# Two MLP groups of two batches recast as 2x2 blocks with Strassen's seven products, and the last expert products of batch 2 at the lowest priority

## The chip, the cores and the metric

The kernel runs on one core of one Trainium2 chip. The metric is the device time of one execution in microseconds (us). TensorE (PE) multiplies matrices into the eight banks of its accumulator memory (PSUM, the tile `bank`); VectorE (DVE), ScalarE (ACT) and GpSimd (POOL) do the elementwise work, and SyncE (SP) issues the transfers. All on-chip data lie in one tile, `arena`.

## The reference, cut to what matters

Three stages follow one another for 4 batches of 448 positions and 768 features: causal attention with 12 heads, an MLP with a low-rank mix over positions, and a top-2 mixture of 4 small attention experts. The change is in the two MLP products.

```python
u  = x + (x^T @ U @ V)^T                       # low-rank mix over the 448 positions
ch = np.maximum(u @ w_ch1, 0.0) @ w_ch2        # 768 -> 3072 -> 768
x  = u + ch
...
out += mask[..., None] * w[:, :, kk:kk + 1] * (a @ v @ wo[e])   # experts
```

## The kernel before, in words

**Numbers.** A float32 value is split into two float16 halves, high and low, and a product of two values is three float16 products (`PASS`: high by high, high by low, low by high). A product of a 768-long contraction is thus 6 blocks of 128 by 3 passes, 18 matmuls of 128x128 by 448 columns into one bank.

**The MLP.** The 3072 hidden features are cut into 4 groups (`NG`) of 6 blocks (`GF`). `mlp(g, bs)` makes the 6 hidden blocks of group g for the batches bs: 18 matmuls each, then ACT applies relu in the bank, ACT casts the high half, DVE subtracts for the low half (`HID`). Then come the 6 output blocks, 18 matmuls each, which DVE adds to the running sum `X3[b]`. Group 2 of batches 2 and 3 is the step `m223`, group 3 the step `m323`: each 24 products of 18 matmuls.

**The weights** come as raw 8-byte words from `in_w1`/`in_w2` (both shown as `in_w_dram`). `weight_tile` decodes each of 48 tiles on DVE, scales it on ACT (high half into a slot of `ring`, full precision in `DEC`), lets POOL make the low half and writes both halves to a scratch tensor in HBM, `W16` (shown as `w`). Later uses reload the tile from there, 384 KB each.

**The steps** stand in the string `ORDER`: `a2` is attention of batch 2, `m02` MLP group 0 of batch 2, `e2` the experts of batch 2. Before, the end of it is `... a3 m02 m12 m223 m323 e2 m03 m13 e3`.

**The order on the engines** is not the order of the code. `Program` records every instruction with a key (`prog.key`); `issue` then runs a list schedule with costs of its own and, on each engine, takes the ready instruction with the lowest key. Attention has low keys; MLP products have `FILL`, the highest, and so fill PE between the attention's products; evacuations have `URGENT`. The experts' products have 0.6e6. The result is one fixed row of instructions on each engine: on the chip each engine waits in that row.

**Scales.** Casts need a power-of-two scale from the largest value. `lowrank` writes a row maximum of each feature block; `split_u` reduces them over the partitions with two small PE products and DVE steps (`reduce_all`) and then casts. Batch 0 uses a bound known beforehand (`CAP`). In `mlp`, the last of group 3 (`g == NG - 1`) takes the maxima anew, which `experts` uses.

Of the kernel before, what the change touches and what calls it, by code (L numbers as in the profile page):

```python
# [23 lines left out]
KD = D // 128  # L24
# [21 lines left out]
SM = 400  # L46
NE = 6
ORDER = "a0 a1 m00 m01 m101 m20 m30 e0 a2 m21 m31 e1 a3 m02 m12 m223 m323 e2 m03 m13 e3"
# [233 lines left out]
def kernel(  # L282
# [40 lines left out]
    bank = banks.tile([128, 8, 512], F32, name="bank")  # L323
    prog.pitch = {bass.MemoryType.SB: total // 4 * 4, bass.MemoryType.PSUM: 8 * 2048}
    W16 = nc.dram_tensor("w16", (NT, 128, 1536), F16, kind="Internal").ap()
    prog.scratch = [W16.tensor]
    BANKS = {"s": (0, 1), "o": (2,), "l": (3, 4), "m": (5, 6, 7), "f": (5, 6), "g": (5, 6, 0, 1), "r": (7,), "x": (5, 6), "y": (2, 7), "b": (3, 4)}
# [7 lines left out]
    def mm(o, lhsT, rhs, start, stop):  # L335
        pe.matmul(o, lhsT, rhs, start=start, stop=stop)
# [21 lines left out]
    def tslot(r, o):  # L358
# [8 lines left out]
        (P32[0:3], PHL[0:2], PT[0:3]), (P32[0:3], PHL[0:2], PT[0:3]),  # L367
# [29 lines left out]
    SCAP = small(1)  # L397
    RF0 = small(NG * GF)
# [193 lines left out]
    def lowrank(n):  # L592
# [19 lines left out]
        if not b:  # L612
            split(UH[0][:, p], UL[0][:, p], X3[0][:, p], SCAP)

    def split_u(b, cast=True):
        t = TMP[:, 7:8]
        dve.tensor_reduce(out=t, in_=AMX[:, b * KD:(b + 1) * KD], axis=AX.X, op=ALU.max)
        reduce_all(t, PU[:, b:b + 1], SU[:, b:b + 1])
# [3 lines left out]
    HT = 4500.0  # L622

    def attention(b):
        if not b:
            prog.key = 0.0
            v_scale(b)
            dve.tensor_tensor(out=CAP, in0=PV[:, 0:1], in1=GAIN, op=ALU.mult)
            dve.tensor_scalar(bits(SCAP), bits(CAP), EXPM, None, op0=ALU.bitwise_xor)
            dve.tensor_scalar(SCAP, SCAP, 2.0 ** 12, None, op0=ALU.mult)  # L630
        for p in range(NP):
# [20 lines left out]
        split_u(b, b > 0)  # L652
# [15 lines left out]
    def weight_tile(i, first):  # L668
# [23 lines left out]
        dve.tensor_scalar(s, s, 2.0 ** 58, None, op0=ALU.mult)  # L692
# [5 lines left out]
        sp.dma_start(out=W16[i], in_=both)  # L698

# [34 lines left out]

    def factors(g):
# [6 lines left out]
        dve.tensor_scalar(TS[:, 7:8], CAP, SU[:, 0:1], 2.0 ** -13, op0=ALU.mult, op1=ALU.mult)  # L742
        dve.tensor_scalar(RF0[:, g * GF:(g + 1) * GF], rf, TS[:, 7:8], None, op0=ALU.mult)

    def mlp(g, bs):

        if 0 in bs:
            factors(g)
# [289 lines left out]
```

## Time and profile before

| What | Value |
|---|---|
| Time, median of 3 runs | 1097.61 us (1097.33 to 1097.76) |
| Span of the profiled execution, first to last instruction | 1094.4 us |
| PE busy | 1064.8 us, 97% of the span |
| DVE, ACT, POOL busy | 607.4, 596.5, 350.4 us |

The profiled execution's own time is known as its span alone; the median stands 3.2 us above it. An engine's busy time is the union of its instructions; matmuls overlap in the pipeline, so the count of matmuls in a stretch tells more than their mean duration. "Idle before" is the engine's idle time just ahead of an instruction, and the name behind it is what ended that time. All instructions of the scheduler bear the line L252, so groups are told apart by shape.

### The profile page before, as it was taken

To read this page: it belongs to the slowest core of one execution; us is meant where nothing else is said; L and a number is where in the kernel's file an instruction comes from. 1 tells how busy PE (TensorE), PEld (TensorE's weight loads), DVE (VectorE), ACT (ScalarE), POOL (GpSimd) and SP (SyncE) were. 2 spreads that over 40 slices of the span, in tenths; PEclk is the share of its full clock that TensorE was granted. 3 is DMA by queue.
4 is the path that set the end of the run, shared out by engine and by line. 5 is a ranking of instruction groups with operands and counts; after the bars stand their busy time and mean duration, and the time that the engine had idled before them with its cause. 6 is when DMAs were issued, how large, how long until landed. Compare 5 with 4: busy or idle time off the path is not lost.

```text
span 1094.4 us, 18802 instructions
## 1 busy us (share of the span) xinstructions
PE 1064.8 (97%) x6932; PEld 568.5 (52%) x6932; DVE 607.4 (56%) x1711; ACT 596.5 (55%) x1445; POOL 350.4 (32%) x411
## 2 busy tenths in 40 slices
PE   8999999999999999999999999999999999999996
PEld 3555554555555555644455644455555555655554
DVE  6788798868786875454546454444112135422253
ACT  3998998666755662567772566762310311731253
POOL 2786767334453420235540225540000000310011
PEclk9999999999999999999999999999999999999998
DMA  5999899647676664449993538984111111555023
GB/s 175 240 242 230 220 208 241 211 164 228 227 234 229 218 242 163 115 120 233 235 202 104 121 112 187 232 170 120 58 58 58 58 58 58 130 134 162 15 41 95
DMA packets 213228, 173.68 MB, mean 159 GB/s; under 512 B 175536, under 2 KB 178736, under 8 KB 213136
## 3 DMA queue, kind: packets, MB, share of 16 engines
q1 hardware_dynamic: 213136, 172.48, 59.2%
q8 instruction: 54, 0.88, 0.3%
q14 instruction: 38, 0.31, 0.1%
HBM read 102.72 MB, written 26.74 MB: 118 GB/s over the span
## 4 chain that ended last, share of the span: by engine, by line
PE 45%; DMA 7%; ACT 3%; DVE 1%; issue 1%; POOL 0%; SPq 0%; POOLq 0%; ACTq 0%
PE bank L252 45%; DMA arena<-arena 7%; ACT arena L252 3%; DVE arena L252 1%; DMA out_dram<-arena 0%; POOL arena L252 0%; ACT bank L252 0%; SPq L252 0%; POOLq L252 0%; ACTq L252 0%
## 5 line engine op out<-in xcount | busy, mean ns | idle before, releaser
L252 PE MATMUL bank<-arena 128*128 128x448 f16 (+10 forms) x6496 | 979.4, 327 | 23.8 <-DMA arena<-arena 11.5
L252 PEld LDWEIGHTS <-arena 128*128 128x128 f16 (+4 forms) x5960 | 486.9, 105 | 433.6 <-issue 81.2
L252 POOL TENSOR_TENSOR arena<-arena 128x384 f16<-128x384 f32 (+6 forms) x400 | 348.2, 891 | 733.5 <-ACT arena L252 708.7
L252 ACT ACTIVATE arena<-arena 112x112 f32<-112x112 f32 (+12 forms) x799 | 433.7, 579 | 228.2 <-DVE arena L252 192.7
L252 DVE TENSOR_TENSOR arena<-bank,arena 128x448 f16<-128x448 f32 (+2 forms) x160 | 95.4, 602 | 190.7 <-ACT arena L252 167.5
L252 DVE CUSTOM_DVE_ANT_0 arena<-bank,arena 112x112 f32<-112x112 f32 (+4 forms) x280 | 125.2, 476 | 71.5 <-PE bank L252 58.1
L252 ACT ACTIVATE bank<-bank,arena 128x448 f32<-128x448 f32 x96 | 57.6, 603 | 178.7 <-PE bank L252 177.6
L252 DVE SCALAR_TENSOR_TENSOR arena<-arena 128x768 int32<-128x768 int32 (+6 forms) x159 | 150.8, 965 | 6.4 <-ACT arena L252 5.7
L252 DVE SCALAR_TENSOR_TENSOR arena<-bank,arena 128x448 f32<-128x448 f32 (+1 forms) x120 | 73.6, 615 | 134.2 <-PE bank L252 113.9
L252 ACT ACTIVATE arena<-bank 128x448 f16<-128x448 f32 (+2 forms) x160 | 82.6, 523 | 45.6 <-PE bank L252 43.5
L252 DVE TENSOR_SCALAR arena<-arena 128x1 int32<-128x1 int32 (+10 forms) x367 | 85.4, 255 | 35.1 <-ACT arena L252 19.5
L991 PE MATMUL bank<-arena 128*128 128x448 f16 x436 | 95.7, 361 | 2.0 <-DVE arena L922 1.0
L252 PEld LDWEIGHTS bank<-arena 64*112 64x112 f32 (+5 forms) x536 | 48.6, 174 | 41.2 <-issue 15.6
L991 PEld LDWEIGHTS <-arena 128*128 128x128 f16 x436 | 40.8, 102 | 46.8 <-issue 14.2
L252 DVE TENSOR_REDUCE arena<-arena 128x1 f32<-128x448 f32 (+6 forms) x107 | 57.8, 545 | 3.8 <-DMA arena<-in_we_dram 2.5
L252 ACT ACTIVATION_READ_ACCUMULATOR arena<-arena 112x1 f32 (+1 forms) x304 | 57.4, 189 | 0.0
L252 ACT ACTIVATE arena<-bank,arena 64x128 f16<-64x128 f32 (+2 forms) x85 | 34.1, 406 | 40.3 <-PE bank L252 37.4
L252 DVE DVE_READ_ACCUMULATOR2_ANT arena<- 112x1 f32 (+1 forms) x280 | 23.0, 82 | 0.1
L252 DVE TENSOR_TENSOR arena<-arena 112x8 f16<-112x8 f32 (+6 forms) x77 | 22.2, 304 | 1.0
L252 DVE CAST arena<-arena 112x8 f16<-112x8 f32 x32 | 14.6, 462 | 2.7 <-PE bank L252 2.5
L252 DVE TENSOR_SCALAR arena<-bank 128x1 f32<-128x1 f32 x48 | 7.3, 152 | 13.5 <-PE bank L252 11.5
L252 DVE COPY arena<-bank 128x1 f32<-128x1 f32 (+2 forms) x14 | 2.2, 158 | 10.0 <-PE bank L252 10.0
(12 smaller groups left out, 18.6 us busy)
## 6 DMA issues: line engine op xcount, KB each, us to landing
arena<-w SPq DMA_DIRECT2D x114, 384.0 KB, 3.2
arena<-in_w_dram SPq DMA_DIRECT2D x48, 768.0 KB, 5.0
w<-arena SPq DMA_DIRECT2D x54, 384.0 KB, 3.6
arena<-in_qk_dram SPq DMA_DIRECT2D x24, 448.0 KB, 4.2
arena<-in_v_dram SPq DMA_DIRECT2D x24, 224.0 KB, 4.5
out_dram<-arena SPq DMA_DIRECT2D x24, 224.0 KB, 2.1
arena<-in_we_dram SPq DMA_DIRECT2D x6, 384.0 KB, 5.8
arena<-arena SPq DMA_TRANSPOSE x88, 4.7
```

Source lines behind the costliest of these rows:

```text
L252: fn(*a, **k)
L991: prog.idle = lambda: nc.tensor.matmul(bank[:, 7, 64:512], ZERO.to_broadcast([128, 128]), ZERO.to_broadcast([128, S]), start=True, stop=True)
```

## The change

**The blocks.** Groups 2 and 3 are done by `strassen(g)` for batches 2 and 3 together. A unit takes two blocks of features by the two batches: the weights are a 2x2 matrix of blocks (even and odd contraction blocks by two output blocks), the activations another (even and odd contraction blocks by batch 2 and batch 3). `seven` makes the four result blocks from seven products of 9 matmuls each (3 contraction pairs by 3 passes) in place of eight. A group has three hidden units and three output units, 63 matmuls each.

**The sums.** Four of the seven need sums of weight blocks (`stationary`: four POOL operations on 128x3x128 elements and two casts a unit, from a full-precision copy `W32` in HBM that `weight_tile` now writes too, for the 24 tiles of these groups) and sums of activations (`operands` for the input, made once; `hidden_unit` for the hidden blocks). `stationary` holds two units' blocks in `ring`.

**The results** are put together on DVE, ACT and POOL: in `hidden_unit` from the banks through `HB` to `BH`, in `output_unit` straight into `X3` and two accumulators.

**Around it.** Batches 2 and 3 share one scale known beforehand (`CAP2`, `SCAP2`), so batch 3 is cast block by block in `lowrank`. Attention of batch 3 gets four buffers in place of two for the transposed weights (`PHL` and two in `hid`). The maxima for the experts are taken by the last group in `ORDER` that adds to a batch (`LAST`): group 3 for batch 2, group 1 for batch 3. The six output products of the experts of batch 2 get the key `2 * FILL`. `ORDER` ends in `... a3 m02 m12 s2 s3 e2 m03 m13 e3`.

```diff
-ORDER = "a0 a1 m00 m01 m101 m20 m30 e0 a2 m21 m31 e1 a3 m02 m12 m223 m323 e2 m03 m13 e3"
+ORDER = "a0 a1 m00 m01 m101 m20 m30 e0 a2 m21 m31 e1 a3 m02 m12 s2 s3 e2 m03 m13 e3"
...
+             "w": (5, 6, 7, 0, 1, 3, 4, 2)}
...
-        (P32[0:3], PHL[0:2], PT[0:3]), (P32[0:3], PHL[0:2], PT[0:3]),
+        (P32[0:3], PHL[0:2], PT[0:3]),
+        (P32[0:3], PHL[0:2] + [hslot("hid", 10752 + 5120 * i) for i in range(2)], PT[0:3]),
...
+        if b == B - 1:
+            split(UH[b][:, p], UL[b][:, p], X3[b][:, p], SCAP2)
...
         sp.dma_start(out=W16[i], in_=both)
+        if g in JOINT:
+            sp.dma_start(out=W32[i], in_=t)
...
-                if g == NG - 1:
+                if (g, b) in LAST:
                     absmax(AMX[:, b * KD + d:b * KD + d + 1], X3[b][:, d])
...
+    def stationary(n):
...
+        for j in range(2):
+            sp.dma_start(out=f[j], in_=W32[i + j])
+        for j in range(2):
+            sp.dma_start(out=a[j].rearrange("p l k m -> p (l k m)"), in_=W16[i + j])
...
+        pool.tensor_tensor(out=o1, in0=e1, in1=o1, op=ALU.add)
+        pool.tensor_tensor(out=e1, in0=e0, in1=e1, op=ALU.subtract)
+        pool.tensor_tensor(out=e0, in0=o1, in1=e0, op=ALU.subtract)
+        pool.tensor_tensor(out=o0, in0=o0, in1=e0, op=ALU.subtract)
+        for j in (1, 0):
...
+            act.activation(hi, f[j], AF.Copy)
+            low(dve, lo, f[j], hi)
...
+        for x, y, out, first in (
+            ("a11", "11", "1", True), ("s1", "t1", "x", True), ("s2", "t2", "y", True),
+            ("a12", "21", "1", False), ("s4", "22", "x", False), ("s3", "t3", "y", False),
+            ("a22", "t4", "z", True),
+        ):
...
+    def hidden_unit(g, u):
...
+            if x == "a11":
+                act.activation(e1, t, AF.Copy)
+            elif x == "s1":
+                act.activation(e5, t, AF.Copy)
+            elif x == "s2":
+                dve.tensor_tensor(out=h12, in0=t, in1=e1, op=ALU.add)
+            elif x == "a12":
+                act.activation(h11, t, AF.Relu, scale=rf[0])
+            elif x == "s4":
+                dve.tensor_tensor(out=h12, in0=t, in1=h12, op=ALU.add)
+                act.activation(h12, h12, AF.Relu, scale=rf[0])
+            elif x == "s3":
+                dve.tensor_tensor(out=e1, in0=t, in1=e1, op=ALU.add)
+                pool.tensor_tensor(out=e5, in0=e5, in1=e1, op=ALU.add)
+                act.activation(e5, e5, AF.Relu, scale=rf[1])
+            else:
+                dve.tensor_tensor(out=h21, in0=t, in1=e1, op=ALU.add)
+                act.activation(h21, h21, AF.Relu, scale=rf[1])
...
+        cut(dve, "11", h11)
+        pool.tensor_tensor(out=t1, in0=h12, in1=h11, op=ALU.subtract)
+        cut(pool, "t1", t1)
+        cut(dve, "22", h22)
+        pool.tensor_tensor(out=t2, in0=h22, in1=t1, op=ALU.subtract)
+        cut(pool, "t2", t2)
+        cut(dve, "21", h21)
+        pool.tensor_tensor(out=t3, in0=h22, in1=h12, op=ALU.subtract)
+        cut(pool, "t3", t3)
+        pool.tensor_tensor(out=t4, in0=h21, in1=t2, op=ALU.subtract)
+        cut(pool, "t4", t4)
...
-        prog.key = base
+        prog.key = 2 * FILL if b == B - 2 else base
         for d in range(KD):
```

The row of POOL, from the end of attention of batch 3 (`128x448` there: low halves of its results) to the first softmax of the experts of batch 2 (`112x112`). Before:

```order
L252 TENSOR_TENSOR arena<-arena 128x448
L252 TENSOR_TENSOR arena<-arena 112x4x112
L252 TENSOR_TENSOR arena<-arena 128x448
L252 TENSOR_TENSOR arena<-arena 112x112 x2
L252 TENSOR_TENSOR arena<-arena 112x2x112 x2
```

The same place after the change, its second group alone: `128x3x128` are the weight sums of `stationary`, `128x448` the sums and low halves of `hidden_unit`, and the last `128x448` the last sums of `output_unit`.

```order
L252 TENSOR_TENSOR arena<-arena 128x448 x7
L252 TENSOR_TENSOR arena<-arena 128x3x128
L252 TENSOR_TENSOR arena<-arena 128x448 x2
L252 TENSOR_TENSOR arena<-arena 128x3x128
L252 TENSOR_TENSOR arena<-arena 128x448 x9
L252 TENSOR_TENSOR arena<-arena 128x3x128
L252 TENSOR_TENSOR arena<-arena 128x448 x6
L252 TENSOR_TENSOR arena<-arena 128x3x128
L252 TENSOR_TENSOR arena<-arena 128x448
L252 TENSOR_TENSOR arena<-arena 128x3x128 x2
L252 TENSOR_TENSOR arena<-arena 128x448
L252 TENSOR_TENSOR arena<-arena 128x3x128 x3
```

Where POOL had nothing between the two steps, the change puts 69 operations of 128x448 and 48 of 128x3x128 in all (of the latter, four already among attention of batch 3); the weight sums of the output units stand among and behind the hidden units' sums.

The row of DVE around the last MLP products of batch 3 (`SCALAR_TENSOR_TENSOR arena<-bank,arena 128x448` adds one to `X3`) and the start of its experts (`SCALAR_TENSOR_TENSOR arena<-arena 128x448` is the low half of a cast, `TENSOR_TENSOR arena<-bank,arena` the first projection's). Before, each sum is followed by its cast:

```order
L252 SCALAR_TENSOR_TENSOR arena<-bank,arena 128x448
L252 SCALAR_TENSOR_TENSOR arena<-arena 128x448
L252 SCALAR_TENSOR_TENSOR arena<-bank,arena 128x448
L252 SCALAR_TENSOR_TENSOR arena<-arena 128x448
L252 TENSOR_TENSOR arena<-bank,arena 128x448 x2
```

After it, the maximum is taken behind each sum, and the reduction over the partitions stands between the last sum and the first cast:

```order
L252 SCALAR_TENSOR_TENSOR arena<-bank,arena 128x448
L252 TENSOR_REDUCE arena<-arena 128x1 x2
L252 TENSOR_REDUCE arena<-bank 1x1
L252 TENSOR_SCALAR arena<-arena 1x1 x2
L252 COPY arena<-bank 128x1
L252 TENSOR_SCALAR arena<-arena 128x1 x6
L252 SCALAR_TENSOR_TENSOR arena<-arena 128x448 x6
L252 TENSOR_TENSOR arena<-bank,arena 128x448 x2
```

The reduction stood far ahead of this place before; now all six casts wait for it. On PE, 30 of the 36 matmuls of the experts' output products of batch 2 stand in this place after the change, around the reduction's two small products, and the other 6 between the first projections of batch 3; before, all 36 stood among the products of group 0 of batch 3.

The row of SP at the same place: `out_dram<-arena` stores the expert results, six for each batch. Before, those of batch 2 stand ahead of the last weight loads:

```order
L252 DMA arena<-w 128x1536 x2
L252 DMA out_dram<-arena 128x448 x4
L252 DMA arena<-w 128x1536 x3
L252 DMA out_dram<-arena 128x448 x2
L252 DMA arena<-w 128x1536 x7
L252 DMA_TRANSPOSE arena<-arena 128x20x112 x4
```

After it they stand behind them, ahead of the last four transposes:

```order
L252 DMA arena<-w 128x1536 x9
L252 DMA out_dram<-arena 128x448 x6
L252 DMA_TRANSPOSE arena<-arena 128x20x112 x4
L252 DMA out_dram<-arena 128x448 x6
```

The stores of batch 2 are the last thing in SP's row before the softmax transposes of the experts of batch 3.

## Rows read from the trace of the kernel before

**Rows 1.** The page: span, busy time of PE, its granted clock in 40 slices.

```profile
span 1094.4 us, 18802 instructions
...
PE 1064.8 (97%) x6932; PEld 568.5 (52%) x6932; DVE 607.4 (56%) x1711; ACT 596.5 (55%) x1445; POOL 350.4 (32%) x411
...
PEclk9999999999999999999999999999999999999998
```

**Rows 2.** Busy time by stretch: length, busy us of each engine (instructions), clock, DMA share, GB/s.

```profile
250.00:400.00 150.00, 149.44 (x825) 80.83 (x823) 118.89 (x261) 96.41 (x154) 66.08 (x57) 1.00 0.70 234
500.00:760.00 260.00, 251.07 (x1849) 132.77 (x1848) 128.04 (x428) 156.02 (x438) 98.09 (x128) 0.99 0.75 174
760.00:1048.00 288.00, 288.00 (x1635) 152.41 (x1633) 86.56 (x200) 75.19 (x161) 13.30 (x18) 1.00 0.27 76
1048.00:1095.00 47.00, 35.95 (x276) 22.12 (x274) 21.43 (x76) 22.36 (x68) 7.79 (x10) 0.89 0.36 79
```

**Rows 3.** Groups of PE by shape between 780 and 880 us.

```profile
L252 PE MATMUL bank<-arena 128*128 128x448 f16 x531 | 100.6, 352 | 0.0
```

**Rows 4.** Timeline of POOL from 700 us: start, duration, idle before.

```profile
747.42 1.03 POOL L252 TENSOR_TENSOR arena<-arena 128x448 f16<-128x448 f32 x1 [9.21 <-ACT arena L252]
937.25 0.40 POOL L252 TENSOR_TENSOR arena<-arena 112x112 f16<-112x112 f32 x1 [188.80 <-ACT arena L252]
```

**Rows 5.** Groups of POOL by shape, 930 to 1094 us: busy, mean ns, idle.

```profile
L252 POOL TENSOR_TENSOR arena<-arena 128x448 f16<-128x448 f32 x4 | 4.1, 1031 | 28.3 <-ACT arena L252 28.3
```

**Rows 6.** Groups of POOL by shape, 210 to 400 us.

```profile
L252 POOL TENSOR_TENSOR arena<-arena 128x384 f16<-128x384 f32 x70 | 80.0, 1163 | 111.1 <-ACT arena L252 109.6 <-PE bank L252 1.4
```

**Rows 7.** Groups by shape over the whole span: DVE and ACT.

```profile
L252 DVE TENSOR_TENSOR arena<-bank,arena 128x448 f16<-128x448 f32 x112 | 68.9, 623 | 145.2 <-ACT arena L252 144.7
L252 DVE SCALAR_TENSOR_TENSOR arena<-bank,arena 128x448 f32<-128x448 f32 x96 | 65.3, 682 | 114.5 <-PE bank L252 113.9
...
L252 DVE TENSOR_TENSOR arena<-arena 112x448 f16<-112x448 f32 x2 | 1.3, 644 | 0.0
L252 DVE SCALAR_TENSOR_TENSOR arena<-arena 128x768 f16<-128x768 f32 x6 | 5.8, 1014 | 0.2 <-ACT arena L252 0.2
...
L252 ACT ACTIVATE arena<-arena 128x768 f16<-128x768 f32 x102 | 89.6, 886 | 53.3 <-DVE arena L252 47.6 <-PE bank L252 5.3
L252 ACT ACTIVATE arena<-arena 128x448 f16<-128x448 f32 x80 | 46.9, 623 | 95.7 <-DVE arena L252 95.4
```

**Rows 8.** The page's DMA issues: engine, count, KB each, median us to landing.

```profile
arena<-w SPq DMA_DIRECT2D x114, 384.0 KB, 3.2
```

**Rows 9.** PE by stretch of 4 us: length, busy (instructions), clock, DMA share, GB/s.

```profile
688.00:692.00 4.00, 1.99 (x26) 1.00 1.20 316
692.00:696.00 4.00, 4.00 (x14) 0.57 0.88 296
```

**Rows 10.** Timeline at the end of group 3, the reduction for the experts of batch 2.

```profile
919.16 0.68 DVE L252 SCALAR_TENSOR_TENSOR arena<-bank,arena 128x448 f32<-128x448 f32 x1 [1.50 <-PE bank L252]
...
923.67 3.46 ACT L252 ACTIVATE arena<-arena 128x448 f16<-128x448 f32 x6 [40.21 <-DVE arena L252]
...
924.74 0.68 DVE L252 SCALAR_TENSOR_TENSOR arena<-arena 128x448 f16<-128x448 f32 x1
```

**Rows 11.** Timeline at the start of the experts of batch 3.

```profile
1046.23 0.68 DVE L252 SCALAR_TENSOR_TENSOR arena<-arena 128x448 f16<-128x448 f32 x1 [0.74 <-ACT arena L252]
...
1049.47 9.14 PE L252 MATMUL bank<-arena 128*128 128x448 f16 x60 [0.72 <-DVE arena L252]
```

**Rows 12.** Timeline of POOL, the low half of the last weight tile.

```profile
394.75 1.79 POOL L252 TENSOR_TENSOR arena<-arena 128x384 f16<-128x384 f32 x2 [2.77 <-ACT arena L252]
```

**Rows 13.** Timeline of DVE, the last sum of group 3 for batch 0.

```profile
429.95 0.68 DVE L252 SCALAR_TENSOR_TENSOR arena<-bank,arena 128x448 f32<-128x448 f32 x1 [2.63 <-PE bank L252]
```

More of the change, by code (lines that the diff above doesn't have):

```diff
@@ L333, in psum, with mm @@
         return bank[:, b[used[kind] % len(b)], :]
[L335 to L336 removed]
+    def mm(o, lhsT, rhs, start, stop, **more):
+        pe.matmul(o, lhsT, rhs, start=start, stop=stop, **more)
     UH = [view("uh", b % 2 * 5376, 128, F16, KD * S).rearrange("p (k s) -> p k s", k=KD) for b in range(B)]
@@ L397 @@
     SCAP = small(1)
+    CAP2 = small(1)
+    SCAP2 = small(1)
+    RF1, RF2 = [small(NG * GF) for _ in range(2)]
+    CF2 = [small(KD) for _ in range(2)]
     RF0 = small(NG * GF)
@@ L651, in attention @@
         lowrank(n)
-        split_u(b, b > 0)
+        split_u(b, b == 1, b < B - 1)
+        if b == B - 2:
+            bound(CAP2, SCAP2, PV[:, 2:3], PV[:, 3:4])
+            for k in range(KD):
+                split(UH[b][:, k], UL[b][:, k], X3[b][:, k], SCAP2)
     ring_n = [0]
@@ new lines, in chain, with cut @@
+    def chain(t, terms, first):
+        more = {} if first else {"skip_group_check": True}
+        prog.key = FILL
+        for i in range(0, len(terms), 3):
+            with prog.group():
+                for j, (l, r) in enumerate(terms[i:i + 3]):
+                    mm(t, l, r, first and i + j == 0, i + j == len(terms) - 1, **more)
+        prog.key = URGENT
+    def hidden_unit(g, u):
+        n = 6 * g + u
+        fs = [g * GF + 2 * u + j for j in range(2)]
+        rf = [RF2[:, f:f + 1] for f in fs]
+        e1, e5, h11, h12, h21 = HB[n % 2]
+        banks_ = {}
+        for x, out, first, terms in seven(n, BU):
+            if first:
+                banks_[out] = psum("w")[:, 0:S]
+            t = banks_[out]
+            chain(t, terms, first)
+            if x == "a11":
[16 more added lines that the diff above has]
+                act.activation(h21, h21, AF.Relu, scale=rf[1])
+        h22, t1, t2, t3, t4 = e5, e1, h11, h12, h21
+        def cut(eng, name, x):
+            hi, lo = BH[name][u]
+            act.activation(hi, x, AF.Copy)
+            low(eng, lo, x, hi)
+        cut(dve, "11", h11)
[9 more added lines that the diff above has]
+        cut(pool, "t4", t4)
@@ L972, in moe @@
             for i in range(NE):
-                k = slot()
-                tiles[48 + i] = halves(k)
-                sp.dma_start(out=view("ring", k * 3072, 128, F16, 1536), in_=W16[48 + i])
+                if b == B - 2 and i > 3:
+                    a = view("stage", (i - 4) * 3072, 128, F16, 1536)
+                    tiles[48 + i] = a[:, 0:768], a[:, 768:1536]
+                else:
+                    k = slot()
+                    a = view("ring", k * 3072, 128, F16, 1536)
+                    tiles[48 + i] = halves(k)
+                sp.dma_start(out=a, in_=W16[48 + i])
         else:
```

172 lines of the change are left out of this document (156 added, 16 removed).

## The prediction

> **What bounds the kernel now.** I read the page first: PE is busy for 1064.8 of 1094.4 us [rows 1], but matmuls overlap in the pipeline, so I asked stretch by stretch whether PE runs at its own pace. The stretches show three kinds of time [rows 2]. From 250 to 400 us PE is full while DVE is at 79% (weights are decoded). From 500 to 760 us, attention of batches 2 and 3, PE idles 260 - 251.07 = 8.9 us. From 760 to 1048 us PE is busy for all 288 us; POOL works 13.3 us of it and the DMA share is 0.27. From 1048 us on, the experts of batch 3, everything waits in turn (PE 35.95 of 47 us).
>
> The change falls into the third stretch: `m223` and `m323` fill most of its first half. The groups of PE from 780 to 880 us show 531 matmuls of 448 columns [rows 3], one per 100 / 531 = 188.3 ns with no idle time before any. A matmul removed there is worth 188.3 ns, as long as what replaces it keeps PE fed. POOL's timeline shows how empty the other side is: between 748.5 and 937.25 us it does nothing for 188.8 us [rows 4].
>
> **The change, part by part.**
>
> *Products.* Before: 2 groups x 24 products x 18 = 864 matmuls. After: 12 units x 7 x 9 = 756. The 108 fewer, at 188.3 ns, are **-20.3 us**. A unit is 63 x 0.1883 = 11.86 us of PE; this is the clock against which the other engines must work.
>
> *DVE and ACT.* A hidden unit gives DVE four sums out of the banks (0.623), three low halves (nearest row 112x448 from arena, 0.644) and two weight low halves (0.644 x 768/448 = 1.10 by elements; a 128x768 cast's low half took 1.01): 6.6 us. An output unit gives it eight sums at 0.682 and two low halves, 7.7 us. ACT has 13 operations near 0.623 and two at 0.886 in a hidden unit, 9.9 us [rows 7]. All lie under 11.86 us, so beside PE: 0 by throughput.
>
> *POOL.* A hidden unit needs nine operations of 448 elements and four of 384: 5568 elements a partition. In the quiet end of the program 448 elements took 1.031 us, 2.30 ns each [rows 5]; in the decode stretch 384 took 1.163, 3.03 ns each [rows 6]. A unit thus costs 12.8 to 16.9 us, against PE's 11.86: POOL is behind by 0.9 to 5.0 us for each hidden unit. An output unit needs the four weight sums alone (four of 384, 3.5 to 4.7 us) and lets POOL catch up. Which rate? DVE was busy 21.43 of 47 us (46%) at the quiet end and 79% in the decode stretch [rows 2]; here 6.6 of 11.86 is 55%, about a quarter of the way: 2.49 ns, 13.9 us a unit, 2.0 us behind. Three units are 6 us late, and two groups 12 us. Much of that is covered: in the order on PE, output products that need only plain casts stand forward among the last hidden ones, and the output units of the first group mix with the hidden units of the second. The second group's output products have nothing behind them but `m03`. I take **+5.0 us**, most of it there; bounds 0 and 6 units x 5.0 = 30.
>
> *Transfers.* A unit loads four tiles of 384 KB; before, one such tile served 36 matmuls, 6.8 us of PE. 1.57 MB in 11.86 us is 133 GB/s, while the decode stretch moved 234 GB/s [rows 2]: no bound by rate. But `ring` holds two units, and a load may start only when the unit before last is done; it lands 3.2 us later [rows 8]. PE's order pulls first products of a unit forward, so I expect two such waits of about 1 us, at the starts of a group and of the output units: **+2.0 us**, bounds 0 and 4 x 3.2 = 12.8 if each switch between hidden and output units shows a whole landing.
>
> *Clock.* Where PE idled for half of 4 us (busy 1.99), the next 4 us were granted 0.57 of full speed, a mix of 1.2 and 2.4 GHz [rows 9]: 4 x 0.43 = 1.7 us lost. The waits above make one such fall likely: **+1.7 us**, bounds 0 and three falls, 5.1.
>
> *Full-precision copies.* 24 writes of 384 KB join the weight stage. DMA there is at a share of 0.70 for 234 GB/s [rows 2]; 9.4 MB at the implied full rate of 334 GB/s is 28 us of the 16 engines, in some 120 us of slack 0.30, so it fits but makes loads later. What hides it is the lead of the weights: the last tile was ready at 396.5 us [rows 12], and its product's sum came at 429.95 [rows 13], 3.4 us of products after its start, a lead of 30 us, or 1.2 us for each of the 24 tiles. **0**; if the cover went, each tile's 1.2 us beyond that would be paid by PE, so I keep 5 as the upper end.
>
> *Attention of batch 3.* Two more buffers, casts that no longer wait for a reduction, and some of POOL's new work standing among its softmax. PE's idle time in the whole stretch is 8.9 us [rows 2]; I take **0**, between -3 and +3.
>
> *The end.* The experts of batch 2 lose 36 matmuls (6.8 us) from the full stretch, and the same 36 stand where batch 3 now waits for its maximum. That wait is priced by the same chain for batch 2: last sum at 919.16, first cast 923.67, its low half done at 924.74 + 0.68 = 925.42, so 6.3 us from the end of the last product [rows 10]. The order puts 30 matmuls there, 5.65 us: about 0.6 us of PE idle is new. Before, that chain ran far ahead, and PE then stood 0.72 us at 1049.47, right after the last low halves [rows 11]; the other six matmuls now stand in that gap. **-0.1 us**, bounds -1 and +6.3 (none fills).
>
> Sum: -20.3 + 5.0 + 2.0 + 1.7 - 0.1 = **-11.7 us**. The profiled span of 1094.4 becomes 1082.7; the median stands 3.2 us above the span, so 1097.6 - 11.7 = **1086 us**.
>
> **The rivals.**
>
> *POOL keeps up.* POOL's total is 69 x 1.03 + 48 x 0.88 = 113 us for 142 us of PE, so on the mean it has room; if the forward products cover all lag, the switch waits stay under 1 us and no clock falls, -20.3 + 2 gives **1079**. For it: 188.8 idle us before. Against: each engine's row is fixed, and the hidden units come in threes.
>
> *POOL is crowded: slower.* If POOL runs here at the 3.03 ns of the decode stretch, six hidden units are 5.0 us behind each, and if the output units' slack does not give it back, -20.3 + 30 is +9.7, **1107**. It decides from 20.3 / 6 = 3.4 us of lag a unit, that is 15.3 us or 2.74 ns an element. For it: 1.163 against 1.031 though the former has fewer elements [rows 5, 6], and DVE's low halves here read two operands from `arena`, as much of the decode work does. Against: DVE is at 55%, not 79%, and half of its work has one operand in a bank. The Trainium skill, "GPSIMD Engine Reference", section "Key points", says that GpSimd shares its SBUF interfaces with VectorE and that they contend where a DVE instruction has two SBUF inputs. By that rule this rival's mechanism is real; the two rows agree in direction, and the profile has no row that prices it at 55%.
>
> *The gain is eaten in the switches.* Three landings of 3.2 us, three clock falls of 1.7 and 5 of POOL are 19.7: **1097**, no change. Each is in the bounds above, but all at once needs every switch to miss.
>
> **How the numbers follow.** The forecast (losses of 5 to 17 us, its own range 1081 to 1093) gets 0.62; POOL keeping up 0.17, the eaten gain 0.08, the crowded POOL 0.13. The predicted time is the forecast's, 1086. The range of 1078 to 1097 leaves out the crowded POOL, nearly half of the eaten gain and a small part of the best case, about 0.2. Within 0.2%, 2.2 us, is what a measurement of this kernel can hardly tell from no change. Faster: 0.62 + 0.17 = 0.79; same 0.08; slower 0.13.
>
> **What would show it.** Right: PE has 108 matmuls fewer; the stretch between attention of batch 3 and the first product of `m03` holds 756 matmuls in 142 us plus 5 to 12 us of idle time, most of it in the second group's output units, ended by DVE's weight low halves or POOL; POOL's means for 448 elements lie at 1.05 to 1.15 us; the reduction before the experts of batch 3 takes 6 us, with under 1 us of PE idle; the weight stage ends within a few us of 397. Wrong: operations of 128x3x128 far from 0.9 to 1.05 us; PE idle in the first hidden units already; a clock below full for more than one stretch of some 3 us there; or PE idle between 300 and 430 us, which would be the copies' price.

## The result, and the profile after

The changed kernel took 1082.5 us (median of four runs, 1079.6 to 1087.6) against 1097.6 us for the kernel before, timed beside it: a ratio of 0.9877, 95% interval 0.9848 to 0.9906, so faster by 15 us. Two later measurements of the same kernel gave 1086.6 us (0.9910, 0.9883 to 0.9938) and 1084.6 us (0.9891, 0.9867 to 0.9915). Its executions spread over 8 us, where those of the kernel before spread over less than 1 in that comparison (5 to 9 in the later ones); the profiled execution below is the slowest of its four, so its span is 8.8 us shorter than that of before, not 15.

The page: span, busy time by engine, and the granted clock in 40 slices. It answers to [rows 1].

```profile
span 1085.6 us, 18934 instructions
...
PE 1043.5 (96%) x6824; PEld 556.0 (51%) x6824; DVE 695.1 (64%) x1811; ACT 639.6 (59%) x1517; POOL 484.7 (45%) x528
...
PEclk9999999999999999999999999999999999999998
```

PE has 6932 - 6824 = 108 matmuls fewer, DVE 88 us more work, POOL 134 us more. Stretch by stretch (length, busy us of each engine, clock, DMA share, GB/s), to be held against [rows 2]:

```profile
250.00:400.00 150.00, 146.31 (x796) 78.36 (x794) 109.84 (x240) 87.39 (x141) 57.85 (x52) 0.99 0.79 267
500.00:760.00 260.00, 251.89 (x1890) 133.22 (x1889) 157.43 (x467) 173.56 (x477) 122.94 (x152) 1.00 0.76 175
760.00:1030.00 270.00, 263.26 (x1499) 138.88 (x1497) 145.47 (x261) 102.23 (x204) 133.53 (x119) 1.00 0.39 117
1030.00:1086.00 56.00, 44.88 (x331) 26.88 (x328) 26.94 (x93) 27.89 (x78) 7.78 (x10) 0.94 0.35 87
```

The reader should see that the full stretch from 760 us on now has 6.7 us of PE idle, and that the weight stage, which had 0.6, has 3.7 with a DMA share of 0.79 instead of 0.70.

To see where time went, I cut PE's row at the last matmul of a stage (the order on PE is fixed, so the n-th matmul belongs to a known step). Lengths in us, worked out from the start and end of those rows in one profile each; the kernels named e1 to e12 are the experiments below:

| kernel | to the end of `a1` | weights: to the end of `m30` | attention 2, 3: to the end of `m12` | groups 2 and 3 of batches 2, 3 | rest | span |
|---|---|---|---|---|---|---|
| before | 214.6 | 215.3 | 329.8 | 164.2 | 170.5 | 1094.4 |
| changed | 216.7 | 221.7 | 326.7 | 145.8 | 174.7 | 1085.6 |
| changed (e1) | 217.9 | 219.2 | 326.5 | 143.6 | 176.8 | 1084.0 |
| changed (e9) | 218.0 | 221.5 | 327.1 | 144.5 | 173.6 | 1084.7 |
| e2, no copies | 214.7 | 213.9 | 327.1 | 144.0 | 174.8 | 1074.5 |
| e3, copies before | 214.2 | 300.0 | 324.6 | 164.3 | 170.2 | 1173.3 |
| e4, early maxima | 217.0 | 220.0 | 325.1 | 146.3 | 171.0 | 1079.4 |
| e5, eighth product | 215.4 | 227.0 | 327.2 | 162.3 | 171.1 | 1103.0 |
| e6, half copies | 217.6 | 214.4 | 326.5 | 143.8 | 174.9 | 1077.2 |
| e7, six buffers | 216.5 | 222.5 | 321.9 | 145.0 | 172.8 | 1078.7 |
| e8, POOL plus | 215.2 | 218.5 | 327.5 | 164.7 | 174.6 | 1100.5 |
| e10, summed back | 219.8 | 214.7 | 329.9 | 162.5 | 179.5 | 1106.4 |
| e11, less POOL | 216.5 | 219.1 | 326.8 | 142.0 | 175.4 | 1079.8 |
| e12, both | 216.7 | 215.4 | 329.0 | 162.8 | 170.7 | 1094.6 |

For the changed kernel's first profile the differences to before are +2.1, +6.4, -3.1, -18.4 and +4.2, together -8.8. The Strassen stretch delivered; the weight stage took a third of it back.

The cuts do not fall on whole steps, because neighbouring steps mix on PE. The column of groups 2 and 3 holds 868 matmuls before, 744 in the changed kernel and 858 in e5. Of the 124 that it has fewer, 108 are gone and 16 stand in other columns: in the changed kernel attention 2, 3 holds 6 more, the rest 13 more, the weights 3 fewer. At 188.3 ns each that is 1.1, 2.4 and 0.6 us of the differences above. PE's own pace for 744 matmuls is 140.1 us; the column of before, with no idle time, took 0.8 us more than 868 x 0.1883 = 163.4.

In the Strassen stretch the groups of PE by shape, 765 to 911 us, have 4.1 us of idle time (before: none, [rows 3]), and the clock stayed at full speed:

```profile
L252 PE MATMUL bank<-arena 128*128 128x448 f16 x745 | 141.9, 353 | 4.1 <-DVE arena L252 2.5 <-DMA arena<-w 1.2 <-ACT arena L252 0.4
```

POOL by shape, 760 to 930 us (before: nothing there at all, [rows 4]):

```profile
L252 POOL TENSOR_TENSOR arena<-arena 128x384 f32<-128x384 f32 x44 | 50.0, 1144 | 15.3 <-DMA arena<-w 14.3
L252 POOL TENSOR_TENSOR arena<-arena 128x448 f32<-128x448 f32 x33 | 44.4, 1355 | 13.6 <-DVE arena L252 13.4
L252 POOL TENSOR_TENSOR arena<-arena 128x448 f16<-128x448 f32 x24 | 27.5, 1157 | 3.2 <-ACT arena L252 3.2
```

A hidden unit costs POOL 5 x 1.355 + 4 x 1.157 + 4 x 1.144 = 16.0 us, far above the 11.9 us of PE, and yet PE waits for 4.1 us in all (2.3 and 3.0 in the profiles of e1 and e9).

In the weight stage the story is on DVE. The first operation that writes into a decode buffer, 216 to 440 us, before:

```profile
L252 DVE TENSOR_SCALAR arena<-arena 128x768 int32<-128x768 int32 x32 | 19.5, 611 | 7.4 <-POOL arena L252 6.0 <-DMA arena<-in_w_dram 1.4
```

and of the changed kernel the same group, with the group of the weight norms' small products on PE:

```profile
L252 DVE TENSOR_SCALAR arena<-arena 128x768 int32<-128x768 int32 x32 | 19.5, 610 | 17.3 <-DMA w<-arena 8.9 <-DMA arena<-in_w_dram 4.5 <-POOL arena L252 3.5
...
L252 PE MATMUL bank<-arena 128*128 128x1 f32 x66 | 9.9, 220 | 5.0 <-ACT arena L252 5.0
```

DVE now waits 8.9 us for `w<-arena`, the stores of decoded weights, because a decode buffer is free only when its full-precision copy has landed. The lead of the finished weights over their use remains: the last low half is done at 411.75 + 1.78 us and its product's sum comes at 438.43, so 21 us are left of the 30 that [rows 12] and [rows 13] show. But the norm of each tile is a product of 128x1 that stands in PE's row among the large ones; when its squares come late, everything behind it waits. The timeline of the changed kernel shows one such moment (start, duration, what, idle before):

```profile
304.07 4.78 SPq L252 DMA_DIRECT2D w<-arena  x4
...
305.72 1.66 ACT L252 ACTIVATE arena<-arena 128x768 f32<-128x768 f32 x2
...
307.27 0.19 ACT L252 ACTIVATION_READ_ACCUMULATOR arena<-arena 128x1 f32 x1
...
307.52 1.70 PE L252 MATMUL bank<-arena 128*128 128x1 f32 x6 [1.73 <-ACT arena L252]
```

PE idles 1.73 us until ACT's accumulator has been read. The windows show what followed (length, busy us, clock, DMA share, GB/s), the picture of [rows 9]:

```profile
304.00:308.00 4.00, 2.27 (x14) 1.10 (x13) 1.04 (x4) 3.97 (x9) 3.06 (x4) 1.00 0.88 291
308.00:312.00 4.00, 4.00 (x14) 1.66 (x13) 2.61 (x7) 2.41 (x3) 1.17 (x2) 0.57 0.73 294
```

After a stretch with PE idle for 1.7 of 4 us, the next was granted 0.57, a mix of 1.2 and 2.4 GHz: 4 x 0.43 = 1.7 us more. PE waits again for norm products at 341.64, 370.62 and 407.64 us. The four waits are 5.0 us together, which is all of PE's idle time in this column; with the clock they are 6.7, against +6.4 in the table. In e1 and e9, with 4.0 and 6.0 us of such waits and no fall of the clock there, it is +3.9 and +6.2.

### The profile page after: what moved, and what is told of

The parts are those of the page before. It is cut to its first block, busy times and chain, and to the rows that moved or that the text cites. A ratio compares the mean times of both kernels' runs of the same rounds, so it can differ in the third digit from the quotient of the medians.

```text
span 1085.6 us, 18934 instructions
## 1 busy us (share of the span) xinstructions
PE 1043.5 (96%) x6824; PEld 556.0 (51%) x6824; DVE 695.1 (64%) x1811; ACT 639.6 (59%) x1517; POOL 484.7 (45%) x528
## 4 chain that ended last, share of the span: by engine, by line
PE 66%; DMA 14%; ACT 8%; POOL 5%; DVE 4%; issue 2%; SPq 0%; DVEq 0%; ACTq 0%; POOLq 0%
PE bank L252 62%; DMA arena<-arena 9%; ACT arena L252 8%; POOL arena L252 5%; PE bank L1248 4%; DVE arena L252 4%; DMA arena<-w 2%; DMA w<-arena 2%; DMA arena<-in_w_dram 1%; DMA arena<-in_wv_dram 1%; DMA arena<-in_v_dram 1%; DMA out_dram<-arena 0%; SPq L252 0%; DMA arena<-in_qk_dram 0%; ACT bank L252 0%
## 5 line engine op out<-in xcount | busy, mean ns | idle before, releaser
L252 PE MATMUL bank<-arena 128*128 128x448 f16 (+10 forms) x6388 | 957.7, 326 | 36.4 <-DMA arena<-arena 12.3
L252 POOL TENSOR_TENSOR arena<-arena 112x112 f16<-112x112 f32 (+8 forms) x517 | 482.5, 956 | 590.7 <-ACT arena L252 544.5
L252 PEld LDWEIGHTS <-arena 128*128 128x128 f16 (+4 forms) x5852 | 474.8, 104 | 430.0 <-issue 82.9
L252 ACT ACTIVATE arena<-arena 128x448 f16<-128x448 f32 (+11 forms) x895 | 492.8, 587 | 272.0 <-DVE arena L252 192.2
L252 DVE SCALAR_TENSOR_TENSOR arena<-arena 128x768 int32<-128x768 int32 (+6 forms) x168 | 163.1, 988 | 2.0 <-ACT arena L252 0.9
L252 DVE SCALAR_TENSOR_TENSOR arena<-bank,arena 128x448 f32<-128x448 f32 (+1 forms) x138 | 84.2, 621 | 88.0 <-PE bank L252 69.2
L252 DVE TENSOR_SCALAR arena<-arena 128x1 int32<-128x1 int32 (+8 forms) x377 | 88.5, 258 | 41.2 <-ACT arena L252 15.6
L252 DVE TENSOR_TENSOR arena<-arena 112x8 f16<-112x8 f32 (+10 forms) x136 | 88.5, 664 | 18.3 <-ACT arena L252 16.7
L252 ACT ACTIVATE bank<-bank,arena 128x448 f32<-128x448 f32 x72 | 43.0, 602 | 53.5 <-PE bank L252 52.2
L252 DVE TENSOR_REDUCE arena<-arena 128x1 f32<-128x448 f32 (+8 forms) x107 | 57.5, 545 | 6.8 <-DMA arena<-in_v_dram 2.9
L252 DVE CAST arena<-arena 112x8 f16<-112x8 f32 x32 | 15.3, 483 | 2.2 <-PE bank L252 1.9
```

The costliest lines, as they stand in the source:

```text
L252: fn(*a, **k)
```

## The experiments

**Theory A:** PE sets the pace of the Strassen stretch, the gain is its 108 missing matmuls, and the full-precision copies cost what the weight stage lost. **Rival P:** POOL sets the pace of that stretch. Each run is put as a ratio to the kernel before on its own chip; e5 to e8 ran on another chip than e1 to e4 and e9 to e12, and the changed kernel was not timed there. e2, e3, e6 and e8 keep the order on every engine; e4, e5, e7 and e10 to e12 were planned anew, so a moved instruction can be part of what they show.

**e1, the changed kernel again**, no edit.

> The changed kernel as it is, timed and profiled again; its four runs lie between 1079.6 and 1087.6 us, and the profiled one is the slowest of them. If the spread comes from the weight stage (the small products that PE waits for there, 5.0 us, and one fall of the clock, 1.7 us, in the first profile), a faster execution shows fewer of these waits, no clock fall before 760 us, and the Strassen stretch (from the last product of group 1 of batch 2 to the last of the second Strassen group) within 1 us of the 145.8 us of the first profile. If the spread comes from POOL in the Strassen stretch, that length varies by several us instead. Median expected 1082 us.

Measured: 1086.6 us, ratio 0.9910 (0.9883 to 0.9938). Waits at the norm products again (4.1 us) and the same gain in the Strassen stretch (143.6).

**e2, no copies.** The write is left out, and the units' loads take other weights:

```
-            sp.dma_start(out=W32[i], in_=t)
...
-            sp.dma_start(out=f[j], in_=W32[i + j])
+            sp.dma_start(out=f[j], in_=we[(i + j) % NE])
```

> Leaves the 24 full-precision copies out; the Strassen units load as many bytes of other data in their place, so the output is not the reference's. All other instructions stand in the same order on every engine. If the copies delay the weight stage and PE waits there for the small norm products (theory A): 5 to 7 us faster than the changed kernel, 1076 us, and no such waits between 250 and 440 us. If the lead of the weights covers the copies, as the prediction said (theory B): within 1 us of the changed kernel, 1082 us.

Measured: 1078.7 us, ratio 0.9836 (0.9812 to 0.9861), so 6.2 us below the mean ratio of the three measurements of the changed kernel (0.9893), and 7.9 below its neighbour e1. The decode's group, 216 to 440 us, no longer waits for stores:

```profile
L252 DVE TENSOR_SCALAR arena<-arena 128x768 int32<-128x768 int32 x32 | 20.9, 654 | 3.0 <-POOL arena L252 2.2 <-DMA arena<-in_w_dram 0.7
```

PE's norm products wait 0.0, and the weight stage takes 213.9 us instead of 219.2 to 221.7. The copies cost 5 to 8 us there.

**e3, the copies put into the kernel before**, each right behind its tile's `W16` write, with that kernel's order kept:

```
         sp.dma_start(out=W16[i], in_=both)
+        if g in (2, 3): sp.dma_start(out=W32[i], in_=t)
```

> The kernel before with the 24 full-precision copies alone, each right behind the tile's other write; nothing reads them. Theory A: 4 to 8 us slower than before, 1102 to 1106 us, PE waiting at the norm products between 250 and 430 us. Theory B (covered by the lead): within 1 us of before, 1098 us.

Measured: 1183.4 us, ratio 1.0802 (1.0772 to 1.0831), more than ten times the expected loss. Waits of DVE and of PE from 216 to 520 us (who waits for what: us in total, times, longest):

```profile
DVE arena L252 <- DMA w<-arena: 91.0, 18, 7.2
...
PE bank L252 <- ACT arena L252: 53.1, 17, 5.6
```

The 53.1 us are all at norm products, and the granted clock was 0.90 over the 300 us of this column, 30 us more. In an order that was made without the copies the next decode stands right behind the release of the buffer, so it waits for whole landings. The changed kernel's order was made with the copies and puts the norm products later in PE's row: the last of them is the 2529th matmul there, against the 2478th here and in the kernel before. The same 24 transfers cost 86 us in one order and 5 to 8 in the other; that the later places are what holds the loss off was read from the two rows and not tried by itself.

**e4, early maxima of batch 3**, so that the moved products need not cover a reduction:

```
-    LAST = {(g, b) for b, g in LAST.items()}
+    LAST = {(NG - 1, b) for b in LAST}
```

> The changed kernel, but the maxima for the experts of batch 3 are taken in the second Strassen group, as the kernel before took them in group 3, so the reduction is out of the chain at the end. The 36 expert products of batch 2 no longer cover that chain and can fill the waits of the experts of batch 3. If the change only swapped one wait for one cover there (the prediction's -0.1 us): 3 to 6 us faster, 1077 to 1079 us, with less PE idle time after the last product of group 1. If the waits of the experts of batch 3 cannot be filled because they stand too late or are too short: within 1 us of the changed kernel.

Measured: 1085.1 us, ratio 0.9895 (0.9867 to 0.9923), 1.5 us below e1 with overlapping intervals. The rest after the Strassen stretch took 171.0 us against 173.6 to 176.8, but e5, without this edit, also took 171.1. Inconclusive.

**e5, an idle eighth product**: `a22` x `t4` once more into a bank that nobody reads.

```
+            ("again", "t4", "q", True),
             ("a22", "t4", "z", True),
```

> The changed kernel with an idle eighth product of nine matmuls put back into each of the twelve units (108 matmuls more, the sum goes to a bank that nobody reads, so the outputs are the same). Theory A (in the Strassen stretch TensorE sets the pace, and the gain is its 108 missing matmuls): 108 x 0.1883 = 20.3 us longer than the changed kernel, 1104 to 1107 us, which is slower than the kernel before by the price of the full-precision copies, 7 to 9 us. Rival P (GpSimd sets the pace there, 15.8 us a hidden unit against 11.9 of TensorE): the added matmuls fall into TensorE's waits, 0 to 10 us longer, 1083 to 1096 us.

Measured: 1098.2 us, ratio 1.0018 (1.0000 to 1.0035) to its before of 1096.2; against the changed kernel's mean ratio that is (1.0018 - 0.9893) x 1097 = 13.7 us. The stretch grew from 143.6 to 145.8 to 162.3 us, that is by 16.5 to 18.7, and for the 858 matmuls that it holds 858 x 0.1883 = 161.6 is PE's own pace. PE by shape, 765 to 930 us:

```profile
L252 PE MATMUL bank<-arena 128*128 128x448 f16 x872 | 165.3, 352 | 0.0
```

With eight products no engine makes PE wait; with seven it waits 2 to 4 us. The whole time missed theory A's range from below by 6 us and the rival's from above by 2; the stretch itself came out close to A's 20.3.

**e6, half copies**: only 384 of the 768 columns are written; the loads are those of e2.

```
-            sp.dma_start(out=W32[i], in_=t)
+            sp.dma_start(out=W32[i, :, 0:384], in_=t[:, 0:384])
```

> The changed kernel, order unchanged, whose 24 full-precision copies hold only half of the columns, 192 KB each; the units load other weights of the same size, so the outputs are not the reference's. With whole copies about 1086 us, without any 1078.7. Theory A (the decode on VectorE waits until the copy has landed and frees the buffer, and a small product in TensorE's row waits for the decode): a shorter landing gives back part of it, some 2 to 5 us, and most of what is left is the fixed part of a landing: 1081 to 1085 us. Rival (the bytes crowd the DMA engines): half of 8 us, 1082 to 1083 us, and the waits for loads, not for buffers, are what shrinks. Rival (the copies cost by their number in SP's row): no change, 1086 us.

Measured: 1079.9 us, ratio 0.9861 (0.9841 to 0.9880), lower than any of the three expectations. The weight stage took 214.4 us, within 0.5 of e2's, and the decode's group reads

```profile
L252 DVE TENSOR_SCALAR arena<-arena 128x768 int32<-128x768 int32 x32 | 20.9, 653 | 7.8 <-DMA w<-arena 2.6 <-POOL arena L252 2.2 <-DMA arena<-in_w_dram 2.1
```

with 0.1 us of waits at PE's norm products. So the number of copies is not the price, and the cost isn't in proportion to the bytes either: the first half is covered, the second half is paid. Both the stores' and the loads' waits fell (from 8.9 and 4.5 us), so this run doesn't tell a buffer that is held too long from crowded transfers.

**e7, six decode buffers** for groups 2 and 3; the order is planned anew, and the copies are whole.

```
+    DEC += [view("p", i * 3072, 128, F32, 768) for i in range(3)]
...
-        n = i % 3
+        n = i % 6 if g in JOINT else i % 3
```

> The changed kernel with six decode buffers instead of three for groups 2 and 3 (three more in space that is free then), all copies kept whole. Theory A (the cost of the copies is the wait for a buffer that a copy still reads): VectorE's waits for w<-arena fall to about nothing, TensorE's waits at the small norm products too, 5 to 8 us less than the changed kernel, 1078 to 1081 us. Rival (bytes and engine time of the transfers): within 1 us of the changed kernel.

Measured: 1081.9 us, ratio 0.9873 (0.9852 to 0.9894), which doesn't tell it from the changed kernel. Its weight stage took 222.5 us (with 9 matmuls more in it, 1.7 us), and PE waits 5.4 us at the norm products: nothing or next to nothing came back. The decode's group:

```profile
L252 DVE TENSOR_SCALAR arena<-arena 128x768 int32<-128x768 int32 x32 | 20.8, 650 | 19.8 <-DMA arena<-in_w_dram 12.0 <-POOL arena L252 3.4 <-DMA w<-arena 2.5
```

The wait for stores went as theory A said (8.9 to 2.5), and the wait for loads took its place (4.5 to 12.0). The median landing of a store issued from 216 to 440 us rose from 4.2 to 5.2 us, and the DMA share from 290 to 410 us from 0.79 to 0.84. More buffers chose another transfer to wait for. But this run does not refute theory A's mechanism (buffer release), because the new order moved the norm products too. The last tile's decode starts at 384.5 us instead of 402.2, so decoding did run ahead; the last norm product, however, is now the 2442nd matmul of PE's row instead of the 2529th, 87 matmuls or 16 us earlier, and PE waits there as before. Six buffers with the norm products left in their places were not tried. What e2 and e6 show, with the order kept, is the place and the price: late decodes at the norm products, 5 to 8 us.

**e8, more work on POOL**: one in-place subtraction of each hidden unit four times over, 3 x 1.36 us more a unit, 24 us in six units. (The subtraction works in place, so its repeats also change the operand `t3`, and the output with it, against what is said of it below.)

```
         pool.tensor_tensor(out=t3, in0=h22, in1=h12, op=ALU.subtract)
+        prog.ops[-1]["calls"] *= 4
```

> The changed kernel with one subtraction of each hidden unit's operands on GpSimd done four times over instead of once (same output): 3 x 1.36 = 4.1 us more of GpSimd in each hidden unit, 6 x 3 x 1.36 = 24 us... counted over the six hidden units with one such subtraction each, three times as much where a unit has three. Theory A (GpSimd has room in the Strassen stretch: 133 us busy of 270): 0 to 5 us longer, 1084 to 1091 us. Rival P (GpSimd's pace is TensorE's pace there): each added microsecond on GpSimd is one of the span, 20 to 75 us longer.

Measured: 1103.5 us, ratio 1.0070 (1.0049 to 1.0091); the stretch took 164.7 us, 19 to 21 more, so most of the added work came out: the 18 added operations are 23 us at the 1.275 us that they took in this run. The granted clock was 0.98 over these 165 us, which is 3 of the 19 to 21 us. PE by shape, 765 to 930 us:

```profile
L252 PE MATMUL bank<-arena 128*128 128x448 f16 x740 | 146.2, 358 | 19.2 <-POOL arena L252 9.8 <-ACT arena L252 5.5 <-DVE arena L252 3.5
```

Rival P was right about the next microsecond: POOL has only some 2 to 4 us to spare, although its busy time in the changed kernel is 120 of 170 us.

**e9, the changed kernel** beside the last three, no edit.

> The changed kernel, nothing altered, beside the three below. Its two medians so far are 1082.5 and 1086.6 us: between these, with waits of 3 to 5 us at the small norm products before 440 us.

Measured: 1084.6 us, as told above, with 6.0 us of waits at the norm products.

**e10, weights summed back** from the two halves on DVE, no copies:

```
-            sp.dma_start(out=f[j], in_=W32[i + j])
+            dve.tensor_tensor(out=f[j], in0=hi, in1=lo, op=ALU.add)
```

> The changed kernel without the full-precision copies: each unit forms its full-precision weights on VectorE as the sum of the two halves that it loads anyway (two sums of 128x768 a unit, 24 in all, some 1.0 us each by the nearest row). Theory A (the copies cost 7 to 8 us in the weight stage through the time of the transfers, VectorE has room in the Strassen stretch, 111 of 170 us busy): waits at the norm products gone, 7 us less than the changed kernel, 1076 to 1080 us. Rival P (GpSimd is within some 5 us of setting the pace there, and VectorE's added work, which reads two operands from SBUF, slows it or stands in the way of the sums out of the banks): the weight stage gains 7 us and the Strassen stretch loses 3 to 10, 1080 to 1088 us.

Measured: 1103.8 us, ratio 1.0077 (1.0049 to 1.0104). The weight stage came back as hoped (214.7 us, no wait at a norm product), and the Strassen stretch lost 18 us, nearly twice the rival's worst. Groups by shape of DVE, POOL and PE, 765 to 930 us:

```profile
L252 DVE TENSOR_TENSOR arena<-arena 128x768 f32<-128x768 f16 x20 | 27.2, 1370 | 1.5 <-DMA arena<-w 1.4
...
L252 POOL TENSOR_TENSOR arena<-arena 128x448 f32<-128x448 f32 x33 | 48.9, 1489 | 13.4 <-DVE arena L252 11.3 <-ACT arena L252 1.8
...
L252 PE MATMUL bank<-arena 128*128 128x448 f16 x761 | 152.4, 360 | 13.0 <-DVE arena L252 8.0 <-DMA arena<-w 3.0 <-POOL arena L252 1.1
```

Each sum took 1.37 us, not 1.0; POOL's means rose (e9: 1324), and PE waits for DVE, which has no idle reserve at the right moments though it is busy only 123 of 165 us. The granted clock was 0.97 over these 165 us, so some 5 of the 18 us are the clock that fell behind the waits. How much is POOL's slower work and how much the longer chain from load to first product isn't settled by this run, nor how much is the new order.

**e11, less on POOL**: `t1` and `t3` of a hidden unit on DVE.

```
-        pool.tensor_tensor(out=t1, in0=h12, in1=h11, op=ALU.subtract)
+        dve.tensor_tensor(out=t1, in0=h12, in1=h11, op=ALU.subtract)
... (t3 likewise)
```

> The changed kernel with two of GpSimd's nine operations on 448 elements in each hidden unit (the differences t1 and t3) given to VectorE: 2 x 1.36 = 2.7 us less of GpSimd a hidden unit, 16 us in all, and 2 x 0.65 = 1.3 us more of VectorE. Theory A (TensorE sets the pace of the Strassen stretch, GpSimd is just inside it): only the waits of 1 to 3 us that are left there can come back, 0 to 3 us less than the changed kernel. Rival P (GpSimd still sets part of the pace): 3 us of waits and more come back, 4 to 8 us less.

Measured: 1082.1 us, ratio 0.9867 (0.9839 to 0.9894), 2.6 us below e9 as theory A said, though the intervals overlap. The stretch took 142.0 us with 0.8 us of idle time on PE, so it is at PE's own pace. Taking 12 operations off POOL (16 us at their mean; its busy time from 765 to 930 us fell from 117.4 to 107.3) gives 2.5; adding 18 (23 us) costs 20. The changed kernel stands at the corner between two bounds.

**e12, the edits of e10, e11 and e4 together.**

> Both edits together (weights summed back on VectorE, two differences taken from GpSimd), and the maxima of batch 3 found a group earlier. Theory A: about 8 to 11 us less than the changed kernel, 1074 to 1078 us, if the parts add up. Rival (VectorE becomes the bound: some 2.0 + 1.3 us more in a hidden unit on top of 6.6, with waits for sums out of the banks): no better than with the sums alone, 1078 us or more.

Measured: 1097.1 us, ratio 1.0009 (0.9992 to 1.0026). DVE is busy 141 of 165 us in the stretch, which took 162.8 us with a granted clock of 0.95 (8 us of it). The parts don't add up: with fewer operations on POOL it took as long as e10, so the sums on DVE decide here.

## Why the prediction was right

The forecast was 1086 us with a range of 1078 to 1097; 1082.5, 1086.6 and 1084.6 were measured. The sum was right, and two of its terms were not: they were wrong in opposite directions by about the same amount. That they cancelled, and that the value came out within 4 us, was luck.

*Products, -20.3.* Right. The stretch shrank by 18.4, 20.6 and 19.7 us, which is 23.3 us for 124 matmuls less all its losses, and putting 108 idle matmuls back (e5, 114 more in the column) gave 16.5 to 18.7 with PE's waits gone.

*POOL +5.0, transfers +2.0, clock +1.7: over-sized.* PE's idle time in the stretch was 4.1, 2.3 and 3.0 us in the three profiles, not 8.7. Its own signs of a slower POOL were there: 448 elements took 1.157 and 1.355 us instead of 1.05 to 1.15, and 128x3x128 took 1.144 instead of 0.9 to 1.05. The two largest waits stood where they were expected (a weight low half of the second group's output units, 1.4 us, and a load at a switch, 0.8 to 1.2 us), and no clock fell there. The step that failed is how lag becomes time. I put POOL at 13.9 us a hidden unit and said that the gain is gone from 15.3 us on. It took 16.0, beyond that bound, and only 2 to 4 us were lost. Lag of one unit is not paid by PE: the six output units need only 4 x 1.14 = 4.6 us of POOL each, so the sum is 6 x 16.0 + 6 x 4.6 = 124 us under PE's 142, and forward products span the rest, as far as the order on PE tells. What decides is POOL's whole row, with the waits that others force on it. From 760 to 930 us, a window 24 us longer than the stretch, the changed kernel's POOL is busy for 120 us and idle for 32 behind loads, DVE and ACT (the three rows above), which leaves little. e8 found the edge some 2 to 4 us further on, and e11 found PE's pace on this side of it. The crowded POOL was a real mechanism, with another price: by an estimate from e8, POOL's work is paid nearly in full from about 16.0 + 3 / 6 = 16.5 us a hidden unit, and at the 19.5 of e8 (8 x 1.275 + 4 x 1.113 + 4 x 1.212, from its rows) the products' gain is gone, as its stretch lies 164.7 - 140.1 = 24.6 us above PE's own pace; at 15.3 it is not.

*DVE and ACT, 0.* Right in the result, though the sum for DVE was too low: its low halves of 448 elements with both operands in `arena` took 999 ns (e9), not the 644 of [rows 7] (two instructions of 112 partitions).

*Full-precision copies, 0 with an upper end of 5.* Wrong: 5 to 8 us, the largest single miss. The failing sentence is that the lead of 30 us hides them. The lead is that of the finished weights before their use. But the decode does not run free: each tile's norm goes through a small product in PE's own row, at a fixed place far ahead of the tile's use, so a late decode stops PE at that place, however long the weights would still have time. The prediction named this sign itself: PE idle between 300 and 430 us "would be the copies' price". e2 and e6 remove those waits with the order kept; e7, with more buffers and a new order, doesn't. My bound of 28 us of DMA time in "120 us of slack 0.30" treated slack as an average; half the bytes fitted (e6), the other half did not.

*Attention of batch 3, 0 (-3 to +3).* -3.1, -3.3 and -2.7 us, but the table misleads here. PE's idle time in this column is the same (9.2 us before, 8.9, 8.5 and 9.2 after). In the one profile of the kernel before the clock fell twice in it, at 692 us [rows 9] and at 536 us (PE: length, busy, clock, DMA share, GB/s):

```profile
532.00:536.00 4.00, 2.25 (x26) 0.95 1.11 214
536.00:540.00 4.00, 4.00 (x23) 0.63 0.69 141
```

At 0.95 and 0.63 over 4 us each that is 0.2 + 1.5 us, and the fall at 692 us is 1.7, so 3.4 together. The changed kernel's three profiles have none there. e3, which keeps the order of before in this column, had none either and took 324.6 us. So the difference is that of two falls in one execution, and the term of 0 held as far as these profiles tell; whether the kernel before falls there more often isn't known.

*The end, -0.1 (-1 to +6.3).* +4.2, +6.3 and +3.1, of which 2.4 are the 13 matmuls more in the column: inside the bounds, wrong in the value taken. The wait that I worked out, PE behind the reduction, is covered. Waits of PE after the Strassen stretch, changed kernel, 911 to 1085 us:

```profile
PE bank L252 <- DVE arena L252: 6.1, 4, 2.0
PE bank L252 <- DMA arena<-arena: 2.7, 2, 2.2
PE bank L252 <- ACT arena L252: 0.7, 1, 0.7
```

and before, 924 to 1094 us:

```profile
PE bank L252 <- DVE arena L252: 4.1, 3, 2.0
PE bank L252 <- DMA arena<-arena: 2.5, 1, 2.5
```

The 2.9 us more are mostly one wait of 1.8 us at 947.72 in the experts of batch 2 and another of 0.8 us ahead of the first product of `m03`. I looked at what the 36 moved products do where they arrive and not at what they had filled where they stood; that this is why the first of these waits is new was argued from the order and not tried by itself.

Before the weight stage the changed kernel was 2.1 to 3.4 us later in its three profiles, in a part that the edits don't touch; e2 and e8, with the same order on PE, were 0.1 and 0.6 us later, e6 3.0. In e1 and e9, 1.7 us of it is one fall of the clock (at 173 and at 81 us); the rest is idle time of PE, spread between executions, of which I know no cause.

## What to carry to other kernels

A lag of one engine behind another is paid only when its whole row, with the waits that others force on it, no longer fits; to find out how near that is, add work to it and see how much comes out, because its busy share (71% here) doesn't tell. And lead of a result hides a late producer only if nothing of the producer's chain stands in the order of the engine that must not wait: look for small instructions of the chain in that engine's row before costing added transfers at nothing. Where a buffer's release is the visible wait, ask which transfer would be waited for next if there were more buffers, and whether the new order leaves the waiting instruction where it stood. Before a difference of a few us between two stages of single profiles is given to a change, hold their falls of the clock and their counts of matmuls against each other.

## What the runs showed of the hardware

The rows fit that POOL and DVE slow each other where DVE reads two operands from `arena`, and not where one of them is in a bank. DVE by shape in e9, 765 to 930 us:

```profile
L252 DVE TENSOR_TENSOR arena<-arena 128x448 f16<-128x448 f32 x18 | 18.0, 999 | 11.1 <-ACT arena L252 11.1
L252 DVE TENSOR_TENSOR arena<-bank,arena 128x448 f32<-128x448 f32 x24 | 14.7, 617 | 7.2 <-PE bank L252 6.8
```

With one operand in a bank the operation takes what the low half took before, 617 against 623 ns [rows 7], with POOL busy all around it; with two in `arena` it takes 999 against 644. POOL's 448 elements with f16 output took 1157 ns against 1031 in the quiet end [rows 5], and with f32 output 1355, for which the kernel before has no row. Where more such work was given to DVE, both rose (POOL's f32 output from 1324 ns in e9 to 1489 in e10, 1496 in e11 and 1456 in e12; DVE's low half from 999 to 1063, 1132 and 1256), while the operation with one operand in a bank stayed at 614 to 617. By the Trainium skill, "SBUF — State Buffer", section "SBUF: two separate sides", the pair of ports that VectorE and GpSimd share is a lock that one instruction holds to its end, and a VectorE instruction with two SBUF inputs takes it against a GpSimd one that reads SBUF; these rows agree in which instructions are slowed.

The other surprise is how much the order decides what a transfer costs: the same 24 stores of 384 KB cost 86 us in one order and 5 to 8 in another.
